# Attention then gMLP on one core: the first batch's attention in two halves of the queries, with gMLP of its first 384 tokens dealt into the second half

## The chip, the cores and the metric

The kernel runs on one core of a Trainium2 chip. The metric is the device time of one execution in microseconds (us). A profiled execution has a span, which was shorter than its time (224.21 and 221.9 us in the profile of the kernel before). TensorE is called PE, VectorE DVE, ScalarE ACT, GpSimd POOL, SyncE SP; PEld is the weight load of PE, and "SPq" is the queue into which SyncE puts transfers.

## The reference

Four batches, eight heads, 768 tokens, head size 64. Block-sparse attention (32-token blocks, a mask over 24 x 24 blocks), then a gMLP with spatial gating on its output.

```python
scores = q @ k.T / sqrt(D)                       # per batch and head, 768 x 768
attn   = softmax(where(mask, scores, -1e9)) @ v  # mask by blocks of 32
x      = attn as (batch, 768, 8 * 64)
h      = relu(x @ w_in)                          # 512 -> 1024
u, v   = h[..., :512], h[..., 512:]
v_n    = (v - mean(v)) / sqrt(var(v) + 1e-6)     # over 512
v_s    = einsum('ts,bsd->btd', w_spatial, v_n) + b_spatial
out    = (u * v_s) @ w_out                       # 512 -> 512
```

The spatial product takes all 768 tokens of a batch, so it must wait for the whole in-projection; the in-projection itself goes by 128 tokens.

## The kernel before

Everything is in bfloat16 on PE. The mask is part of the score product: rows 64 to 87 of a transposed key or query ("mask rows") hold a block indicator and the mask's row, so that 88 rows are contracted in place of 64. The scores come out transposed (keys on partitions), so the exponential feeds the value product directly. One pass of the main loop is a *slot*: two score matmuls, one exponential of 128x768, six value matmuls for a slot seven passes older. A head takes six slots, a pair of heads twelve, a batch 48.

```python
def qk_exp(j, ci):                                # head j, key chunk ci
    ps = psum.tile([128, 1024], FP32, tag="sc", bufs=2)
    for hf in range(2):                           # both halves of the queries
        nc.tensor.matmul(out=ps[:, hf * 512:hf * 512 + HALF],
                         lhsT=kt[j % 4][:, ci * 128:(ci + 1) * 128],
                         rhs=qt[j % 4][:, hf * HALF:(hf + 1) * HALF], ...)
    nc.scalar.activation(out=a_ref[j][:, ci, :]..., in_=ps..., func=AF.Exp, scale=0.125)

for p in range(NP + 1):                           # 16 pairs of heads
    for s in range(12):
        qk_exp(j, ci)
        ...                                       # transposes of pair p + 1
        if p == 0 and s == 0:
            cast_v(0); prepare(1); load(2); load_weights(2)
        if s == 7 and p + 2 < NP:
            if p + 3 < NP:
                load(p + 3)                       # three transfers of 0.39 MB
            ...
            prepare(p + 2)                        # POOL casts keys, queries, values to bf16
        if s == 10 and NG + 1 < p + 2 < NP:
            tr_dma(p + 2, "k"); tr_dma(p + 2, "q")  # transposes by DMA, same SPq
        ...                                       # from p = 5 on DVE copies the halves of pair p + 1, s = 5 and 9
        while moe_q and budget >= 0.5:            # gMLP matmuls of the batch before
            moe_q.popleft()(); budget -= 1
        if g >= LAG: av(...)
        if s == 8 and p >= NG:
            xtr(p - 1)
            if p % NG == 0:
                moe_q.extend(moe_units(p // NG - 1))   # 108 matmuls of 128x512
```

The mask rows of heads 1 to 3 are copied by DVE, and later heads reuse the same four tiles, mask rows included. All loads but the first two (the keys of heads 0 and 1, which ACT issues), all DMA transposes (keys, attention output, spatial weights, gates) and all stores are put into the one SP queue in program order.

The softmax here doesn't subtract the row's maximum and nothing guards it: scores larger than these inputs give would overflow.

## Time and profile before

| | before |
|---|---|
| time, median of 4 runs (lowest to highest) | 223.41 us (223.16 to 223.70) |
| span of the profiled execution | 221.9 us |
| mean granted clock of PE | 0.996 to 1.0 |

Two lines of the page of the kernel before that the prediction doesn't show. Each digit is a fortieth of the span (5.5 us): busy tenths of PE, then the granted clock of PE in tenths (9 is 90% or more).

```profile
PE   7999999999999999999999999999999999999993
...
PEclk9999999999999999999999999999999999999999
```

After the first slice PE is busy for nine tenths or more of every slice but the last, and the trace's clock record stays at 1.0 from 6.3 to 221.3 us. The second view is the table by stretches of the same trace, for the start; the columns are: stretch and its length, busy us and number of instructions of PE, PEld, DVE, ACT and POOL, granted clock, DMA share, GB/s.

```profile
9.00:10.50 1.50, 1.08 (x8) 0.63 (x7) 0.38 (x2) 1.50 (x3) 1.01 (x2) 1.00 0.15 49
10.50:12.00 1.50, 1.50 (x19) 1.04 (x17) 0.55 (x1) 1.33 (x3) 1.36 (x2) 1.00 0.00 0
```

From 9 to 12 us the DMA engines do next to nothing (shares 0.15 and 0.00). The old start could wait with its next loads: pair 2 was not needed before slot 24.

### The profile page before, as it was taken

What the parts mean: (1) busy time and instruction counts of PE and PEld (TensorE: products, weight loads), DVE (VectorE), ACT (ScalarE), POOL (GpSimd) and SP (SyncE); (2) the same over time, 40 slices, a digit from 0 to 9 for tenths busy, and PEclk for the clock granted to TensorE, in tenths of its full rate; (3) what the DMA queues carried; (4) which work ended last, traced back from release to release, by engine and by line L of the source; (5) the groups of instructions that cost most, each with busy time, mean ns of one, the idle gap of its engine ahead of it and who ended that gap; (6) DMA issues with size and microseconds to landing.
All of it is one profiled execution on the core that took longest, in us unless ns stands there. A gap on an engine that the chain in (4) does not pass through costs nothing.

```text
span 221.9 us, 5325 instructions
## 1 busy us (share of the span) xinstructions
PE 214.8 (97%) x2154; PEld 130.2 (59%) x2154; DVE 127.8 (58%) x282; ACT 177.1 (80%) x246; POOL 64.0 (29%) x88
## 2 busy tenths in 40 slices
PE   7999999999999999999999999999999999999993
PEld 3567777775656565665656555566656655544541
DVE  5566454557868545268867544559675433666531
ACT  5699999998899888888899878888989884265351
POOL 5436760439905701210606102110501000022000
PEclk9999999999999999999999999999999999999999
DMA  6679989996799886999774378998141124710015
GB/s 197 229 250 370 393 300 327 366 149 73 204 279 180 252 120 171 212 294 285 239 154 168 68 114 243 188 300 234 24 85 35 34 41 89 257 48 0 0 60 225
DMA packets 56092, 40.25 MB, mean 181 GB/s; under 512 B 39300, under 2 KB 51588, under 8 KB 56068
## 3 DMA queue, kind: packets, MB, share of 16 engines
q1 hardware_dynamic: 55780, 39.53, 67.7%
q10 hardware_dynamic: 288, 0.39, 0.6%
q8 instruction: 16, 0.26, 0.5%
q14 instruction: 8, 0.07, 0.1%
HBM read 24.38 MB, written 6.29 MB: 138 GB/s over the span
## 4 chain that ended last, share of the span: by engine, by line
PE 81%; ACT 14%; DVE 2%; issue 1%; POOLq 0%; POOL 0%
PE ps_moe L386 31%; PE ps L290 23%; ACT a_all L294 13%; PE ps_av L306 13%; PE ps_t L386 6%; PE ps_sc L386 3%; PE wps L180 2%; PE ps L228 1%; PE ps_x L330 1%; PE ps_g L434 1%; POOLq L567 0%; DVE gn L441 0%; DVE stats L399 0%; PE ps_tr L239 0%; ACT vsb L394 0%
## 5 line engine op out<-in xcount | busy, mean ns | idle before, releaser
L294 ACT ACTIVATE a_all<-ps 128x768 bf16<-128x768 f32 x192 | 149.5, 814 | 19.3 <-PE ps L290 10.7
L290 PE MATMUL ps<-qt,kt 88*128 88x384 bf16 x384 | 93.6, 325 | 1.8 <-ACT a_all L294 0.6
L306 PEld LDWEIGHTS <-a_all 128*128 128x128 bf16 x1152 | 60.4, 97 | 37.0 <-issue 0.4
L306 PE MATMUL ps_av<-vv,a_all 128*128 128x65 bf16 x1152 | 67.9, 194 | 0.0
L386 PE MATMUL ps_moe<-w_in_t,xt 128*128 128x512 bf16 x144 | 42.1, 378 | 0.0
L386 PE MATMUL ps_moe<-vn,w_spt 128*128 128x512 bf16 x108 | 31.8, 378 | 0.0
L290 PEld LDWEIGHTS <-kt 88*128 88x128 bf16 x384 | 28.2, 98 | 4.7 <-issue 1.9
L386 PEld LDWEIGHTS <-xt 128*128 128x128 bf16 x192 | 18.6, 97 | 16.1 <-issue 0.3
L112 POOL CAST vv<-st_v 128x768 bf16<-128x768 f32 x16 | 13.2, 828 | 47.3 <-PE ps_av L306 42.5
L441 DVE SCALAR_TENSOR_TENSOR gn<-ps_moe,b_col,un 128x512 bf16<-128x512 f32 x18 | 13.5, 748 | 18.6 <-PE ps_moe L386 18.5
L403 POOL TENSOR_SCALAR std<-mv 128x3 f32<-128x3 f32 x8 | 2.2, 277 | 72.2 <-DVE mv L400 59.5
L386 PE MATMUL ps_moe<-w_out_t,gt 128*128 128x512 bf16 x72 | 20.6, 378 | 0.1
L386 PEld LDWEIGHTS <-w_spt 128*128 128x128 bf16 x144 | 13.7, 97 | 11.4 <-issue 0.9
L399 DVE BATCH_NORM_STATS2 stats<-vsb 128x6 f32<-128x512 bf16 x24 | 16.7, 694 | 3.3 <-ACT vsb L394 2.7
L320 DVE TENSOR_TENSOR xn<-ps_av,rc 128x384 bf16<-128x384 f32 x32 | 17.8, 557 | 1.1
L396 DVE TENSOR_SCALAR vsb<-ps_moe 128x512 bf16<-128x512 f32 x18 | 12.4, 689 | 10.3 <-PE ps_moe L386 10.3
L109 POOL CAST nat_k<-st_k 128x768 bf16<-128x768 f32 x15 | 12.4, 825 | 17.4 <-DMA st_k<-in_k_dram 9.4
L319 DVE RECIPROCAL rc<-ps_av 128x6 f32<-128x6 f32 x32 | 6.0, 188 | 15.9 <-PE ps_av L306 15.8
L386 PEld LDWEIGHTS <-gt 128*128 128x128 bf16 x96 | 8.8, 97 | 6.9
L109 POOL CAST nat_q<-st_q 128x768 bf16<-128x768 f32 x15 | 12.5, 833 | 0.0
L409 DVE TENSOR_SCALAR vn<-vsb,mv,rstd 128x512 bf16<-128x512 bf16 x24 | 10.3, 447 | 2.6 <-POOL rstd L405 2.5
L279 DVE COPY kt<-tt_k 64x768 bf16<-64x768 bf16 x20 | 8.5, 425 | 4.2 <-DMA tt_k<-nat_k 4.1
(80 smaller groups left out, 172.7 us busy)
## 6 DMA issues: line engine op xcount, KB each, us to landing
st_v<-in_v_dram SPq DMA_DIRECT2D x16, 384.0 KB, 5.7
out_dram<-osb SPq DMA_DIRECT2D x24, 256.0 KB, 2.5
st_q<-in_q_dram SPq DMA_DIRECT2D x15, 384.0 KB, 3.8
st_k<-in_k_dram SPq DMA_DIRECT2D x15, 384.0 KB, 4.8
wst<-in_moe_w_spatial_dram SPq DMA_DIRECT2D x3, 768.0 KB, 8.5
wst<-in_moe_w_in_dram SPq DMA_DIRECT2D x4, 512.0 KB, 8.9
wst<-in_moe_w_out_dram SPq DMA_DIRECT2D x2, 512.0 KB, 7.2
st_k<-in_k_dram ACTq DMA_DIRECT2D x2, 192.0 KB, 3.0
```

Of the source, the lines that this page charges most:

```text
L109: eng.tensor_copy(out=dst, in_=src)
L112: nc.gpsimd.tensor_copy(out=vv[p % 3][:, :, :, 0:D], in_=st.pop(("v", p)).rearrange("p h (c d) -> p h c d", d=D))
L279: nc.vector.tensor_copy(out=(qt if nm == "q" else kt)[(2 * p + h) % 4][0:D, :], in_=src[h * D:(h + 1) * D, :])
L290: nc.tensor.matmul(out=ps[:, hf * 512:hf * 512 + HALF], lhsT=kt[j % 4][:, ci * 128:(ci + 1) * 128], rhs=qt[j % 4][:, hf * HALF:(hf + 1) * ...
L294: nc.scalar.activation(out=a_ref[j][:, ci, :].rearrange("p (b c) -> p b c", b=2), in_=ps.rearrange("p (b c) -> p b c", b=2)[:, :, 0:HALF], ...
L306: nc.tensor.matmul(out=av_ref[j][:, qc, :], lhsT=a_ref[j][:, ci, qc * 128:(qc + 1) * 128], rhs=vv[p % 3][:, h, ci, :], start=(ci == 0), st ...
L320: nc.vector.tensor_tensor(out=xn_ref[p][:, :, h, :], in0=ps[:, :, 0:D], in1=rc.to_broadcast([128, NCH, D]), op=ALU.mult)
L386: nc.tensor.matmul(out=box[0], lhsT=lhs, rhs=rhs, start=(i == 0), stop=(i == n - 1))
L396: nc.vector.tensor_scalar(out=vsb[:, tcc, :], in0=ps, scalar1=0.0, scalar2=None, op0=ALU.max)
L399: nc.vector.bn_stats(out=stats, in_=vsb[:, tcc, :])
L409: nc.vector.tensor_scalar(out=vn[:, tcc, :], in0=vsb[:, tcc, :], scalar1=mv[:, tcc, 0:1], scalar2=rstd[:, tcc:tcc + 1], op0=ALU.subtract, ...
L441: nc.vector.scalar_tensor_tensor(out=gn[:, tcc, :], in0=ps, scalar=b_col[:, tcc:tcc + 1], in1=un[:, tcc, :], op0=ALU.add, op1=ALU.mult)
```

## The change

The intent: the first batch is bound by ACT, and PE has gaps in it. If the eight heads are run for the first 384 queries, then for the second 384, three token chunks of the attention output are ready after 24 slots. Sixteen matmuls of the in-projection can then fill gaps of PE in the first batch, and so leave the stage that PE bounds.

```diff
+    def qk_exp_half(g):                           # 3 slots a head, 24 slots a half
+        gh, i = divmod(g, NCH // 2)
+        grp, j = divmod(gh, H)
+        ...
+        for u in range(2):
+            ci = 2 * i + u                        # two key chunks, one half of the queries
+            nc.tensor.matmul(out=ps[:, u * 512:u * 512 + HALF],
+                             lhsT=kt[j][:, ci * 128:(ci + 1) * 128],
+                             rhs=qt[j][:, grp * HALF:(grp + 1) * HALF], ...)
     ...
-    qt = [const.tile([KR, S], BF16, name=f"qt{s}") for s in range(4)]
+    qt_all = const.tile([KR, H, S], BF16)         # all eight heads of a batch are kept
+    qt = [qt_all[:, h] for h in range(H)]         # (keys and values likewise)
     ...
-        gt = work.tile([128, NCH, NDH, 128], BF16, tag="gt", bufs=2)
+        gt = work.tile([128, NCH, NDH, 128], BF16, tag="gt", bufs=1)
     ...
+        order = ("v0 v1 u0 v2 u1 u2 v3 v4 u3 v5 u4 u5" if b == 0 else
+                 "v0 v1 v2 v3 v4 v5 u0 u1 u2 u3 u4 u5" if last else
+                 "v0 v1 u0 v2 u1 v3 u2 v4 u3 v5 u4 u5")    # before: v0 v1 v2 u0 v3 u1 ...
     ...
+    for t in (kt_all, qt_all):                    # mask rows of heads 2 to 7, SBUF to SBUF
+        nc.sync.dma_start(out=t[D:KR, 2:H, :],
+                          in_=t[D:KR, 0:1, :].to_broadcast([NB, H - 2, S]))
+    load(2, "kq")
+    load_weights(1)
+    load(2, "v")
+    load(3, "kq")
+    load_weights(1)
+    load(3, "v")
     ...                                           # the first batch has a loop of its own:
+    for g in range(N0):                           # 48 slots
+        qk_exp_half(g)
+        for p, nm, third in tr_slots.get(g, ()):  # transposes of pairs 1 to 4
+            tr_pair(p, nm, third)
+        ...
+        if g == 30:
+            moe_q.extend(moe_units(0))
+        if g in (31, 32, 33, 34, 42, 43, 45, 46):
+            moe_q.popleft()()
+            moe_q.popleft()()
+        first_batch_rest(g)                       # value matmuls, 4 slots behind
```

## The prediction

> **What bounds the kernel now.** I speak of slots: one slot is one pass of the main loop, with two score matmuls (keys by queries), one exponential over 128x768, and six value matmuls for an older slot. Each batch has 48 slots, 192 in all; the gMLP of a batch is 108 matmuls of 128x512, dealt one to three at a time into the slots of the next batch.
>
> I read the page first: its busy shares and its 40 slices.
>
> ```profile
> PE 214.8 (97%) x2154; PEld 130.2 (59%) x2154; DVE 127.8 (58%) x282; ACT 177.1 (80%) x246; POOL 64.0 (29%) x88
> ...
> ACT  5699999998899888888899878888989884265351
> ```
>
> On average TensorE (PE) looks like the bound, but a mean mixes stages. ACT is at nine tenths in slices 3 to 9, so I asked for the busy time of each engine in two stretches, the first batch and the one after it.
>
> ```profile
> core 0: us, PE busy (x) PEld busy (x) DVE busy (x) ACT busy (x) POOL busy (x), PEclk, DMA share, GB/s
> 18.00:48.00 30.00, 29.41 (x408) 22.27 (x406) 15.25 (x32) 29.77 (x42) 13.70 (x16) 1.00 1.01 328
> 51.00:75.00 24.00, 24.00 (x247) 14.39 (x246) 18.46 (x40) 21.49 (x31) 15.82 (x15) 1.00 0.98 197
> ```
>
> In the first, ACT has no room; PE's 29.41 is modelled ends, not work. The chain that ended last says which engine times each stage (start, duration, what):
>
> ```profile
> 30.77 4.21 ACT a_all L294 x6
> 35.02 4.21 ACT a_all L294 x6
> ...
> 50.92 0.33 PE ps L290 x2
> 51.25 0.65 PE ps_moe L386 x3
> 51.90 0.19 PE ps_av L306 x6
> 52.09 0.33 PE ps L290 x2
> 52.42 0.43 PE ps_moe L386 x2
> 52.85 0.19 PE ps_av L306 x6
> ```
>
> Up to about 50 us the exponentials follow each other every 4.21/6 = 0.70 us, whereas PE needs 0.33 + 0.19 = 0.52 us a slot, and 0.11 more where two transposes lie in it. From 50 us on PE is the chain without a gap: score pair 0.33, value group 0.19, gMLP matmul 0.215 each (0.65/3). So the kernel is **ACT-bound for 57 slots, PE-bound after that**, to the end. A gMLP matmul moved from the second stage into an empty place of the first saves 0.215 us.
>
> How empty is the first stage? These are three successive slots of its timeline:
>
> ```profile
> 47.51 0.49 PE L290 MATMUL ps<-qt,kt 88*128 88x384 bf16 x2
> 47.83 0.36 PE L306 MATMUL ps_av<-vv,a_all 128*128 128x65 bf16 x6
> 48.21 0.49 PE L290 MATMUL ps<-qt,kt 88*128 88x384 bf16 x2
> ```
>
> A score pair is complete 0.49 after its start, an exponential alone takes 0.81, and there are two score buffers. So scores of slot n may start when exponential n-2 ends: 0.49 + 0.81 + some 0.05 of signalling = 1.35, against two periods of 0.705 = 1.41. PE can therefore run late by only some 0.06 us before ACT waits.
>
> [...]
>
> **The change part by part.**
>
> The first batch's 48 exponentials stay 48 of 128x768, but two key chunks by 384 queries in place of one by 768. So all heads' first halves are ready after 24 slots, and 16 gMLP matmuls (value columns of three token chunks, gate columns of one) can lie in slots 31 to 34, 42, 43, 45, 46.
>
> (a) Those 16 leave the PE-bound stage: 16 x 0.2155 = 3.45 us saved. In the first stage such a slot takes 0.33 + 0.19 + 0.43 = 0.95 on PE, 0.246 over the exponential's 0.706. Eight times 0.246 = 1.97, less 0.06 of room in each of three runs, is 1.8 us paid. Net gain **1.65**. It is nothing else than eight idle gaps of 0.185 filled.
>
> (b) The rest is dealt from slot 54 on, where before it began in slot 57. Before, the scores of slots 54 and 57 started at 47.51 and 49.80, with the six transposes of the fourth pair (0.33) between. PE's own work there is 3 x 0.52 = 1.56, and the transposes now lie in ACT-bound slots. Gain 2.29 - 1.56 = **0.7**. A 0.25 us gap of ACT at 43.6, for a probability buffer, should go too, as value matmuls now follow at 4 slots in place of 7: **0.2**.
>
> (c) Start: a head now takes three slots, so pairs 1 to 3 must be loaded, cast and transposed by slot 18. Slots 0 to 3 carry 12 to 14 small transposes and fillers more than an exponential covers; working them through, each loses 0.15 to 0.3, and exponential 6 starts at some 13.2, as before. Before, slot 12 lost a further 0.45 to a query copy. Gain **0.2**. The loads: 2.36 MB of the first two pairs, 0.44 of mask rows copied in SBUF, then keys and queries of pair 2, one weight piece, values 2, keys and queries of pair 3: 5.3 MB. At 328 to 374 GB/s from 2.2 us on that lands between 16.4 and 18.4, and the cast (0.83) follows; slot 13 comes at 18.2. Loss **0.3** as a mean of none and 0.6.
>
> (d) The instruction order shows a new wait. The second-half in-projection of slot 42 takes the PSUM buffer that the transposed queries of the next pair have just filled in slot 41; two copies of 0.56 must empty it. The copies end 0.44 + 0.2 + 1.12 = 1.76 after that slot's start; PE would be there after 1.13. So 0.6 to 0.7 is lost, and in slot 54 again 0.75, by the same order. Loss **1.4**.
>
> (e) One relu (0.48 behind an exponential, half covered) joins ACT in its own stage, and slots 8, 10, 14, 16 and 41 hold 0.03 to 0.1 too much transposing: loss **0.4**.
>
> (f) The remaining 92 matmuls over 51 slots make 0.52 + 1.8 x 0.2155 = 0.91 us a slot, where before it was 1.0. ACT needs 0.706 plus a relu of 0.48 every 2.2 slots in the in-projection, 0.92. The two are level there, and with two buffers that costs a little: loss **0.3**.
>
> (g) The last gMLP does all value columns first. Before, PE waited there 0.20 us for the normalised values; gain **0.2**. Eight more normalisations on DVE (8 x 0.3) and the single gate-transpose buffer are off the path: DVE was 51% busy from 18 to 48 us.
>
> Sum: 1.65 + 0.7 + 0.2 + 0.2 + 0.2 = 2.95 gained; 0.3 + 1.4 + 0.4 + 0.3 = 2.4 lost. Net 0.55. The slot list looks tuned by hand, so I trust the losses a little less than the gains and choose 1.5: **222.0 us**.
>
> **The rivals.** *The saving comes whole.* If PE had more room in the first stage than 0.06 us of lateness allows, the move would give up to 3.45 + 0.9, and the time would be near 219. For it: PE's 0.52 against 0.70. Against it: each burst holds four or two slots in a row, and only two score buffers exist.
>
> *A copy takes the place of the wait.* If the copies behind the query transposes queue up behind others on DVE, each costs over 1 us, and the gain is gone: 223.5 or more. For it: the order in (d). Against it: DVE is idle half the time.
>
> *The loads become the bound.* All four pairs must be there by 18 us. A late pair stalls PE and ACT together; 2 us late makes 224 to 225. For it: the DMA share is near 1 from 8 us on. Against it: the first 10 us carry the same bytes, sorted better (keys before values), and the weights come after.
>
> **Range and chances.** Of the gains, (a) and (b) are near certain; (c) to (f) each may be off by 0.5 to 1. Together some 1.6 us either way: 219.8 to 224.3. Over 2% faster needs 4.5 us, more than (a) and (b) can give without losses: 0.04. Over 2% slower needs a load over 4 us late: 0.02. Within 2%: 0.94.
>
> **What would show it.** In the changed kernel's chain, ACT should carry the slots up to 30; PE and ACT should mix in 31 to 46. The scores of slot 54 should start between 48.5 and 50 us (47.51 before). The waits list should show PE or its weight loads waiting for a query copy, about 0.6 us, twice. The row of exponentials should keep its 192 and 814 ns. From slot 54 to the end PE should be without gaps beyond 0.5 us in sum. I am wrong if PE waits for loads before 20 us for over 1 us, if exponentials stay 0.70 apart through slots 31 to 46 (then the saving is whole), or if the PE-bound stage shows gaps for weights or transposed gates.

## The result, and the profile after

| | before | after |
|---|---|---|
| time, median of 4 runs | 223.41 us (223.16 to 223.70) | 231.26 us (229.47 to 232.37) |
| ratio of the fast runs | | 1.034 [1.027, 1.042] |
| mean granted clock | 0.996 to 1.0 | 0.984 to 0.993 |

A ratio is the mean time of one kernel's fast runs over that of the other's fast runs of the same rounds, so it is not quite the ratio of the medians quoted; a 95% interval stands in brackets. The change made the kernel **slower by 3.4%**, outside the range of the prediction.

The page of the changed kernel:

```profile
PE 215.5 (95%) x2154; PEld 129.7 (57%) x2154; DVE 136.5 (60%) x297; ACT 178.1 (78%) x247; POOL 64.5 (28%) x89
...
PE   7979999998999999979999799999999999999992
...
ACT  5677999898999889886989678888999885266351
PEclk9997999999999999999999999999999999999999
```

The work is the same (215.5 us busy against 214.8), but PE has weak slices where it had none: slices 3, 10, 18 and 23; and in slice 4 the granted clock falls to seven tenths on average. ACT is less full in slices 3 and 4. The two stretches that the prediction read, of the changed kernel:

```profile
18.00:48.00 30.00, 28.96 (x360) 20.25 (x359) 17.38 (x49) 27.74 (x39) 12.04 (x14) 0.96 0.82 297
51.00:75.00 24.00, 23.26 (x248) 14.26 (x245) 20.72 (x35) 22.40 (x33) 19.36 (x17) 1.00 0.83 168
```

ACT has lost 2.0 us of the first (27.74 against 29.77) and PE, which had no gap in the second, 0.74. Where is it lost? I cut the execution at the starts of exponentials number 31 and 54. These starts are read from the trace; the forecast by stage is the prediction's own sum, divided among the stages by me ((c) and half of (e) to the first; the payment in (a), the first wait of (d), the other half of (e) and the ACT gap of (b) to the second; the rest to the third).

| | start to slot 31 | slots 31 to 54 | slot 54 to the end | span |
|---|---|---|---|---|
| before | 31.5 | 16.6 | 173.8 | 221.9 |
| forecast | 31.8 | 19.05 | 170.5 | 221.35 |
| after | 34.8 | 19.0 | 173.9 | 227.7 |

The middle is as forecast to within 0.1 us. In part that is luck: going by the middle stages of e9_late (18.3) and e14_nodeal (16.3) below, the gMLP slots cost 2.0 us where 1.8 was forecast and the wait 0.7 where 0.65 was, and the stage without either is 0.3 us shorter than before, where no difference was forecast. The profiled execution lost 3.0 us more than forecast in the start and 3.4 us in the long stage, where the saving should have come in. (The other three runs took 1.1 to 2.9 us longer than the profiled one; more on the clock below.)

**The start.** The same table by stretches as for before:

```profile
9.00:10.50 1.50, 1.50 (x16) 1.01 (x15) 1.47 (x3) 1.20 (x2) 0.83 (x1) 1.00 1.04 201
10.50:12.00 1.50, 1.47 (x20) 1.07 (x18) 1.35 (x4) 1.13 (x2) 0.83 (x1) 1.00 0.99 152
12.00:13.50 1.50, 1.35 (x22) 0.96 (x19) 1.44 (x3) 1.50 (x3) 0.46 (x1) 1.00 1.07 214
13.50:15.00 1.50, 0.81 (x10) 0.52 (x10) 0.12 (x2) 0.76 (x2) 0.37 (x1) 1.00 1.07 362
15.00:18.00 3.00, 2.28 (x27) 1.62 (x26) 1.38 (x4) 2.03 (x3) 1.65 (x2) 0.79 1.04 384
18.00:21.00 3.00, 3.00 (x35) 2.29 (x34) 2.00 (x6) 2.16 (x3) 2.21 (x3) 0.64 1.05 387
```

From 9 to 13.5 us the DMA engines are full (share 0.99 to 1.07), yet move only 152 to 214 GB/s; afterwards they move 362 to 387 at the same share. In the slow stretch the mask rows are being copied from SBUF to SBUF (the two transfers are put into the queue at 6.55 and 7.62 us, and PE's wait for them ends at 14.19). Then the clock: 0.79 and 0.64 on average, and the trace's clock record has 0.5 from 16.73 to 20.14 us. What PE waited for, from its timeline (start, duration, what, idle time before and what ended it):

```profile
14.19 0.48 PE L319 MATMUL ps<-qt_all,kt_all 88*128 88x384 bf16 x2 [0.83 <-DMA qt_all<-qt_all]
...
15.91 0.28 PE L242 MATMUL ps_tr<-ident,nat_k 128*128 128x128 bf16 x2 [0.72 <-POOL nat_k L110]
...
44.10 0.60 PE L432 MATMUL ps_moe<-w_in_t,xt 128*128 128x512 bf16 x2 [0.53 <-DVE qt_all L247]
...
54.33 0.60 PE L432 MATMUL ps_moe<-w_in_t,xt 128*128 128x512 bf16 x2 [0.63 <-DVE qt_all L247]
...
91.44 0.59 PE L432 MATMUL ps_moe<-w_out_t,gt 128*128 128x512 bf16 x2 [0.78 <-DVE gn L490]
...
102.63 0.51 PE L376 MATMUL ps_x<-ident,xn 128*128 128x128 bf16 x6 [1.33 <-DVE xn L366]
...
127.52 0.38 PE L432 MATMUL ps_moe<-vn,w_spt 128*128 128x512 bf16 x1 [0.86 <-DVE vn L455]
128.35 0.38 PE L432 MATMUL ps_moe<-vn,w_spt 128*128 128x512 bf16 x1 [0.45 <-DVE vn L455]
```

The first wait is for the mask rows of slot 6, the second for the cast keys of pair 2. The two at 44 and 54 us are the waits for query copies that the prediction foresaw. The last four, 3.42 us in sum, are those that the long stage lacks.

**The long stage.** The waits at 91 and 103 us name DVE. So I looked at what DVE did just before the second of them:

```profile
101.16 0.72 DVE L273 COPY kt_all<-tt_k 64x768 bf16<-64x768 bf16 x2 [3.12 <-DMA tt_k<-nat_k]
...
102.02 0.56 DVE L366 TENSOR_TENSOR xn<-ps_av,rc 128x384 bf16<-128x384 f32 x1
```

DVE had been standing for 3.12 us in front of a copy of transposed keys (tt_k) that had not landed; the normalisation that PE needed came after it in program order. The chain that ended last shows what held the keys:

```profile
84.60 4.68 DMA tt_k<-nat_k
...
91.83 4.16 DMA st_k<-in_k_dram
...
96.27 4.87 DMA tt_k<-nat_k
```

A load (put into the queue at 91.83), its cast, then the transpose of the keys: transfers are on the path, in a stage in which PE alone was expected there. The load came late because it stood in the SP queue behind transposes of gates, keys and queries (issued from 83.2 to 91.2 us), which themselves waited for DVE and POOL: from 74 to 92 us the queue had waits of 2.1 and 1.7 us for DVE's key and query copies and of 1.9 us for a cast of POOL. In the waits list POOL's wait for keys grew from 9.4 us (6 times, longest 4.6) before to this:

```profile
POOL nat_k L110 <- DMA st_k<-in_k_dram: 39.6, 6, 15.6
...
DVE kt_all L273 <- DMA tt_k<-nat_k: 8.0, 3, 3.1
```

The wait at 127 us is of another kind. The in-projection's new order puts the value columns of the last chunks later, so they are normalised later. DVE then does one normalisation (0.90 us from 123.95), two copies of keys (1.87 from 124.76) and two more normalisations (1.65 from 126.65), and PE, which goes straight on to the spatial product, waits for these.

### The profile page after: what moved, and what is told of

Same layout as the page of the kernel before. It is cut to its first block, busy times and chain, and to the rows that moved or that the text cites.

```text
span 227.7 us, 5347 instructions
## 1 busy us (share of the span) xinstructions
PE 215.5 (95%) x2154; PEld 129.7 (57%) x2154; DVE 136.5 (60%) x297; ACT 178.1 (78%) x247; POOL 64.5 (28%) x89
## 4 chain that ended last, share of the span: by engine, by line
PE 66%; DMA 11%; DVE 6%; issue 6%; ACT 4%; POOL 4%; SPq 1%; POOLq 0%; ACTq 0%
PE ps_moe L432 23%; PE ps L284 14%; PE ps_av L300 8%; DMA st_k<-in_k_dram 7%; PE ps_t L432 7%; PE ps L319 6%; DMA tt_k<-nat_k 4%; PE ps_sc L432 3%; PE ps_av L335 3%; ACT a_all L323 3%; DVE kt_all L273 1%; ACT a_all L288 1%; POOL nat_k L110 1%; PE ps_tr L242 1%; DVE vn L455 1%
## 5 line engine op out<-in xcount | busy, mean ns | idle before, releaser
L284 PE MATMUL ps<-qt_all,kt_all 88*128 88x384 bf16 x288 | 70.3, 325 | 0.1
L300 PEld LDWEIGHTS <-a_all 128*128 128x128 bf16 x864 | 46.1, 97 | 34.9 <-issue 1.1
L432 PE MATMUL ps_moe<-w_in_t,xt 128*128 128x512 bf16 x144 | 42.7, 378 | 1.2 <-DVE qt_all L247 1.2
L432 PE MATMUL ps_moe<-vn,w_spt 128*128 128x512 bf16 x108 | 32.5, 378 | 1.3 <-DVE vn L455 1.3
L432 PEld LDWEIGHTS <-xt 128*128 128x128 bf16 x192 | 18.4, 97 | 17.4 <-DVE qt_all L247 1.9
L319 PE MATMUL ps<-qt_all,kt_all 88*128 88x384 bf16 x96 | 24.3, 335 | 1.4 <-DMA qt_all<-qt_all 0.8
L490 DVE SCALAR_TENSOR_TENSOR gn<-ps_moe,b_col,un 128x512 bf16<-128x512 f32 x18 | 13.5, 748 | 17.1 <-PE ps_moe L432 17.1
L455 DVE TENSOR_SCALAR vn<-vsb,mv,rstd 128x512 bf16<-128x512 bf16 x24 | 17.7, 768 | 4.9 <-POOL rstd L451 4.9
L284 PEld LDWEIGHTS <-kt_all 88*128 88x128 bf16 x288 | 19.3, 98 | 0.6 <-issue 0.2
L113 POOL CAST vv<-st_v 128x768 bf16<-128x768 f32 x16 | 13.5, 842 | 16.7 <-PE ps_av L335 9.9
L335 PEld LDWEIGHTS <-a_all 128*128 128x128 bf16 x288 | 15.2, 100 | 4.7 <-issue 0.2
L366 DVE TENSOR_TENSOR xn<-ps_av,rc 128x384 bf16<-128x384 f32 x24 | 13.4, 558 | 0.8
(91 smaller groups left out, 221.3 us busy)
```

The source lines that it names most:

```text
L113: nc.gpsimd.tensor_copy(out=vv[p % NG][:, :, :, 0:D], in_=st.pop(("v", p)).rearrange("p h (c d) -> p h c d", d=D))
L284: nc.tensor.matmul(out=ps[:, hf * 512:hf * 512 + HALF], lhsT=kt[j % H][:, ci * 128:(ci + 1) * 128], rhs=qt[j % H][:, hf * HALF:(hf + 1) * ...
L300: nc.tensor.matmul(out=av_ref[j][:, qc, :], lhsT=a_ref[j][:, ci, qc * 128:(qc + 1) * 128], rhs=vv[p % NG][:, h, ci, :], start=(ci == 0), s ...
L319: nc.tensor.matmul(out=ps[:, u * 512:u * 512 + HALF], lhsT=kt[j][:, ci * 128:(ci + 1) * 128], rhs=qt[j][:, grp * HALF:(grp + 1) * HALF], s ...
L335: nc.tensor.matmul(out=av_ref["half", gh][:, qc, :], lhsT=a_ref["half", gh][:, ci, qc * 128:(qc + 1) * 128], rhs=vv[p][:, h, ci, :], start ...
L432: nc.tensor.matmul(out=box[0], lhsT=lhs, rhs=rhs, start=(i == 0), stop=(i == n - 1))
```

## The experiments

Eighteen kernels ran, in five lots, each lot on one chip together with runs of the kernel before. Ratios are to the kernel before in the same lot. Four repairs come up several times; I name them here:

- *loads*: from pair 9 on the loads are put into the queue five slots earlier.
- *order*: the in-projection order of before (v0 v1 v2 u0 v3 ...) for the second and third gMLP.
- *transposes*: those of pairs 4 and 5 are dealt one slot earlier at their end, so that their copies are over before the gMLP wants the PSUM buffer.
- *mixed start*: mask rows of heads 2 and 3 by four DVE copies, those of heads 4 and 5 by transfers behind the keys of pair 2, those of 6 and 7 behind the keys of pair 3, and the first weight piece after that.

### First lot: where the losses are

**a_again**: the changed kernel once more.

> The changed kernel itself, on the chip of the three experiments beside it. Theory: 6 to 9 us slower than before; a low-clock stretch of about 3.4 us (one or two of them) at half the clock before 25 us, and TensorE gaps of 0.8, 1.3 and 1.3 us near 91, 103 and 128 us. If the low clock were an accident of the first chip, this run would lack it and be only some 4 us slower than before.

It took 231.13 us, 1.034 [1.030, 1.039], with the wait for mask rows now 2.29 us and the late waits within 0.3 us of those above. The result stands; the size of the wait at the start varies from run to run.

**e1_mask**: mask rows of heads 2 to 7 by twelve DVE copies in place of the two transfers.

```diff
-    for t in (kt_all, qt_all):
-        nc.sync.dma_start(out=t[D:KR, 2:H, :], in_=t[D:KR, 0:1, :].to_broadcast(...))
+        if g in (3, 5, 8, 11, 14, 17):
+            j = (3, 5, 8, 11, 14, 17).index(g) + 2
+            for t in (kt, qt):
+                nc.vector.tensor_copy(out=t[j][D:KR, :], in_=t[0][D:KR, :])
```

> Mask rows of heads 2 to 7 by twelve small vector copies in place of the two SBUF-to-SBUF transfers. Theory (the two transfers hold the queue from 9.5 to 13 us at half its rate, so mask rows and the keys of pair 2 come late, TensorE idles, and its clock is halved): the 0.8 and 0.7 us waits go, keys of pair 2 land near 12.5 instead of 15 us, no half-clock stretch, the scores of slot 12 start near 18 instead of 20.6 us, and the time falls by 3 to 5 us. Rival (the loads themselves are too many for the first 18 us, the transfers matter little): under 1 us.

It took 230.65 us, 1.029 [1.023, 1.035]. Its profiled run fell in the slow state, so of it I use only what was waited for and when keys were cast, not the length:

```profile
15.43 0.50 PE L319 MATMUL ps<-qt_all,kt_all 88*128 88x384 bf16 x2 [0.98 <-DVE qt_all L568]
...
26.32 0.34 PE L356 MATMUL ps_x<-ident,xn 128*128 128x128 bf16 x3 [1.65 <-DVE xn L347]
```

The keys of pair 2 were now cast at 11.92, 3.1 us earlier, but the copies made DVE the one that PE waits for. A miss in its effect (0.5 us off a_again's median, where 3 to 5 were expected), yet it shows that the transfers held the keys of pair 2. The keys of pair 3 came no earlier: cast at 20.25, against 19.47 in the changed kernel.

**e2_fill**: four matmuls of 512 columns on zeros before each of the two early waits, so that PE is not idle there.

> The transfers stay; four filler matmuls of 512 columns stand before each of the two early waits, so TensorE is busy while it waits. If the halved clock comes of the idle stretch at 13 to 16 us: full clock throughout, the waits themselves remain, and the time falls by 1.3 to 3 us. If the clock is lowered by something else (the rise of all engines' load, or chance): the half-clock stretch stays and the time rises by 0 to 1 us.

It took 229.53 us, 1.029 [1.024, 1.033]. The clock was 0.996 to 1.0 in all four runs, against 0.981 to 0.993. The stretch that had 0.79 (the next, with 0.64 before, has 1.00 too):

```profile
15.00:18.00 3.00, 2.53 (x26) 1.44 (x25) 0.54 (x2) 1.51 (x2) 1.28 (x2) 1.00 1.04 386
```

So **the halved clock follows from PE's idle time at the start** (1.55 us of the 3.4 us ahead of it in the changed kernel), and is worth about 0.5% (1.034 to 1.029, 1.2 us; the intervals overlap). It is a consequence, not the first cause.

**e3_loads**: the *loads* repair alone.

```diff
-                if p + 3 < NP:
+                if p + 3 < NP and p < 6:
                     load(p + 3)
+            if s == 2 and p >= 6 and p + 3 < NP:
+                load(p + 3)
```

> From the seventh pair on, the loads of a pair are issued five slots earlier, ahead of the transposed stores of gated rows in the same queue. Theory (loads stand behind those in the queue, the transposed keys come late, VectorE waits for them in order, and TensorE for VectorE): the TensorE gaps near 91 and 103 us (0.8 and 1.3) go, the start stays as it is, and the time falls by 2 us. Rival (the transfers of this stretch are simply too many, the order is no matter): the gaps move elsewhere, the time stays within 0.5 us.

It took 229.72 us, 1.026 [1.021, 1.032]. The waits at 91 and 103 us are gone, and DVE's wait for transposed keys fell from 8.0 to 1.5 us, as the theory says. The waits at 127 and 128 us are still 0.86 and 0.45. The time fell by 1.4 us from a_again, where 2 was expected.

### Second lot: the other late waits, and the dealing itself

**e4_order**: the *order* repair alone.

> The in-projection order of the second and third gMLP as in the kernel before (three value chunks ahead of the first gate chunk, and three gate chunks after the last value chunk, in place of two and two). Theory: the TensorE gap near 128 us (0.86 + 0.45, normalised values not there) goes, as 4 more matmuls stand between the last value chunk and the spatial product; the time falls by 1.3 us. Rival (the values are late because of the key copies on VectorE and the casts on GpSimd, not the order): the gap stays or moves, under 0.4 us.

It took 229.87 us, 1.024 [1.017, 1.031]. No PE wait is left at 127 us; those at 91 and 102 us stay. That settles this pair of waits.

**e5_tr**: the *transposes* repair alone.

```diff
-                     (3, (13, 14, 14, 15, 16, 16)), (4, (36, 37, 38, 39, 40, 41))):
+                     (3, (13, 14, 14, 15, 16, 16)), (4, (36, 37, 37, 38, 39, 40))):
```

(and in the same way for pair 5)

> The transposes of the fifth and sixth pair end one slot earlier, so that their copies out of PSUM are over when the in-projection wants the buffer. Theory: the waits of 0.53 and 0.63 us near 44 and 54 us go and the time falls by 1.0 to 1.4 us. Rival (ACT is the bound there and takes the gap anyway): under 0.4 us.

It took 231.03 us, 1.031 [1.026, 1.036]. The waits of 0.53 and 0.63 us at 44 and 54 us are gone, but its profile has a longer wait at the start than any other:

```profile
17.13 0.80 PE L319 MATMUL ps<-qt_all,kt_all 88*128 88x384 bf16 x2 [3.66 <-DMA qt_all<-qt_all]
```

So the time of this run says little about the repair; the waits do.

**e6_nodeal**: no gMLP in the first batch; all 108 matmuls from slot 54 on.

```diff
-        if g in (31, 32, 33, 34, 42, 43, 45, 46):
-            moe_q.popleft()()
-            moe_q.popleft()()
```

> No gMLP in the first batch: all 108 matmuls of the first gMLP are dealt from slot 54 on; the halves stay. By the prediction's own sum the 16 moved matmuls are worth 3.45 - 1.8 - 0.7 - 0.25 = 0.7 us, so the scores of slot 54 start 2.7 us earlier and the time rises by 0.7. If the moving is also what causes the late transposed keys at 91 and 103 us (everything of the first gMLP stands earlier in the transfer queue), those 2 us come back and the time falls by 1 to 1.5 us. If the moved matmuls lay in idle time for nothing, the time rises by 3 us.

It took 231.21 us, 1.033 [1.025, 1.041]: no different from the changed kernel. The waits at 91 and 103 us are gone here too (the gMLP is not ahead, so the keys are in time), those at 128 us are not. That the dealing was worth nothing here does not yet say what it is worth when nothing stands in its way (e14).

**e8_split**: the mask rows of heads 2 and 3 first, those of heads 4 to 7 behind the keys of pair 2.

> The mask rows of heads 2 and 3 alone go ahead of the loads of pair 2, those of heads 4 to 7 behind its keys and queries. No work is added to VectorE. Theory (the two transfers run at half rate and hold up the first rows and the keys behind them): the wait before slot 6 falls from 0.8 to 2.3 us to under 0.5, the keys of pair 2 land 1.5 to 2 us earlier, the scores of slot 12 start 1.5 to 2.5 us earlier, one or both half-clock stretches go, and the time falls by 2 to 4 us. Rival (the bytes have to come through before slot 12 anyway): the wait moves to slots 7 to 13, under 1 us.

It took 230.91 us, 1.032 [1.025, 1.038]. The wait before slot 6 is gone, but the one for cast keys has moved on to pair 3 and is longer:

```profile
22.55 0.29 PE L242 MATMUL ps_tr<-ident,nat_k 128*128 128x128 bf16 x2 [2.81 <-POOL nat_k L110]
```

Splitting the transfers moves the loss and does not take it away, as long as four heads' mask rows and a weight piece stand ahead of the keys of pair 3.

### Third lot: repairs together

**e9_late**: *loads*, *order* and *transposes*; the start as changed.

> The three repairs behind slot 36 together (loads earlier, old in-projection order, transposes a slot earlier); the start as changed. If the losses add, ratio 1.034 - 0.008 (loads) - 0.008 (order) - 0.003 (transposes) = 1.015, or 227 us, and no TensorE gap over 0.3 us after 40 us. What is then left over the kernel before, some 3.5 us, is the start alone, and the scores of slot 54 start 3 to 5 us later than before's 47.5. If the repairs overlap (the same time, counted twice), ratio over 1.02.

It took 227.7 us, 1.014 [1.006, 1.023]. After 40 us PE has no wait over 0.42 us. At the start it waits 2.71 us for mask rows and 0.86 for cast keys. So the late repairs give about 3.4 us (231.1 to 227.7, over two lots).

**e10_latemask** and **e11_latemask_all** (results wrong): scores of heads 2 to 7 with 64 rows, that is without mask rows in the first pass, and the two transfers not issued until slot 34; in the second with the three late repairs.

> Wrong results on purpose: in the first batch heads 2 to 7 are taken without the mask rows (64 rows in place of 88), and the two transfers that make them run at slot 34, for the later batches. This takes the transfers out of the start without giving VectorE anything. Theory (the transfers are what delays the start): no wait before slot 6, keys of pair 2 cast near 12.5 us, full clock, scores of slot 12 near 18 us, time down by 3 to 4 us. Rival (the loads of pairs 2 and 3 are too many for the time whatever the mask rows do; in e1_mask the keys of pair 3 landed at 20.2 us without the transfers): a wait for the keys of pair 3 at slot 13 of 1 to 2 us, time down by 1 to 2 us only.

> Wrong results on purpose, as e10_latemask, with the three repairs of e9_late. What the change would be worth if the mask rows cost nothing. By the prediction's sum with (d), the late loads and the in-projection order taken out: 223.4 - 2.9 + 0.7 = 221 us, if the start is no slower than before. If the start still loses 2 us to the loads: 223.

They took 230.88 us, 1.030 [1.019, 1.041], and 227.17 us, 1.012 [1.002, 1.021]. The granted clock was 1.0 in their profiles, but PE took longer for a slot with score matmuls of 64 rows: in e10_latemask, at 12.3 us, a score pair and a value group take 0.41 and 0.30 us from start to start, in place of the 0.33 and 0.19 of 88 rows (slots 0.84 to 0.95 apart from 13 to 18 us). So the gain of the start was lost in another way, and for the time these two are inconclusive. The rival's sign did come in e10_latemask: without any mask rows in the start PE still waited 1.01 us for the cast keys of pair 3, cast at 18.79. For the cause they are useful all the same. The trace records each packet of a transfer; loads and mask rows go in packets of 1536 bytes. Their median duration:

| stretch | before | after | e2_fill | e10_latemask | mixed start (e12) |
|---|---|---|---|---|---|
| 8 to 10 us | 65 ns | 65 | 65 | 65 | 65 |
| 10 to 12 us | none | 155 | 160 | 65 | 65 |
| 12 to 14 us | 65 | 98 | 141 | 65 | 65 |
| 14 to 16 us | 65 | 68 | 75 | 65 | 65 |
| 30 to 32 us | 66 | 65 | 66 | 193 | 68 |

The long packets go where the six-head transfers go: at 10 to 14 us in the changed kernel, at 30 to 32 us where they are issued at slot 34. **While the mask rows are copied, the median packet takes 1.5 to 3 times as long.** In the changed kernel 421 of the 661 packets of this size from 9 to 14 us took over 100 ns (before: 10 of 385). The mask rows are only 288 packets (2 transfers of 216 KB), so at least 133 of the long ones belong to loads. Summed over the packets between 6 and 26 us that took over 100 ns, the excess over 65 ns is 2.3 us of all 16 engines in the changed kernel (2.9 in its second profile) and 0.6 us before. The sum alone does not decide the start: it is 1.6 in e12_mix and 2.4 in e13_xfer below, whose starts are repaired.

**e12_mix**: *mixed start* with the three late repairs.

```diff
+    def mask_dma(h0):
+        for t in (kt_all, qt_all):
+            nc.sync.dma_start(out=t[D:KR, h0:h0 + 2, :],
+                              in_=t[D:KR, 0:1, :].to_broadcast([NB, 2, S]))
     load(2, "kq")
-    load_weights(1)
+    mask_dma(4)
     load(2, "v")
     load(3, "kq")
+    mask_dma(6)
+    load_weights(1)
     ...
+        if g in (1, 5):
+            j = 2 if g == 1 else 3
+            for t in (kt, qt):
+                nc.vector.tensor_copy(out=t[j][D:KR, :], in_=t[0][D:KR, :])
```

> Right results. Mask rows of heads 2 and 3 by four vector copies, those of 4, 5 and 6, 7 by transfers of two heads each, behind the keys of pair 2 and of pair 3; a weight piece moves behind the keys of pair 3; the three repairs of e9_late. If the start can be repaired by order: 1.5 to 2.5 us better than e9_late, near 224.5 us. If bytes and not order are the limit of the start: within 0.7 us of e9_late.

It took 223.89 us, 1.000 [0.991, 1.009], with a right result: 1.5% less than e9_late of the same lot, from the start alone. Keys of pair 2 were cast at 11.58 (after: 15.03), those of pair 3 at 17.75 (after: 19.47). PE was left with these waits over 0.3 us:

```profile
97.27 0.51 PE L376 MATMUL ps_x<-ident,xn 128*128 128x128 bf16 x6 [0.71 <-DVE xn L366]
```

and 0.76 us at 13.44 for a query copy, and 0.63 at 109.11 for a relu of DVE.

### Fourth lot: what of the start, and what the dealing is worth

**e13_xfer**: as e12_mix, but the mask rows of heads 2 and 3 by two-head transfers ahead of the keys of pair 2, not by DVE.

> As the mixed version (1.000 of before), but the mask rows of heads 2 and 3 come by two two-head transfers ahead of the keys of pair 2, not by four VectorE copies. If what matters is how many bytes stand ahead of the keys (0.15 MB here, 0.44 MB in the changed kernel), it stays within 0.3% of the mixed version, near 224. Rival, the start is repaired by taking the transfers of mask rows away from in front of the keys altogether: 225.5 or more, with a wait for cast keys of over 1 us before slot 6 or 12.

It took 224.84 us, 1.002 [0.996, 1.007]. That is within the noise of e12_mix; the longest wait for cast keys is 0.60 us, so the rival with over 1 us falls. It does not take DVE: two heads' mask rows may stand ahead of the keys. What this does not separate is the weight piece (0.52 MB, more than the mask rows' 0.44), which the *mixed start* also moves behind the keys of pair 3; no run moves it alone.

**e14_nodeal**: as e12_mix, without gMLP matmuls in the first batch.

> The mixed version without gMLP matmuls in the first batch: all 108 from slot 54 on. By part (a) of the prediction the dealing is worth 1.65 us net once nothing else is in the way, so this should be 1.65 us slower than the mixed version of the same sort, near 225.5 (1.007 of before). Rival, the dealing is worth nothing (the slots of the first batch with gMLP pay for it all): equal, 223.9. Second rival, the saving is whole: 227.3.

It took 224.46 us, 0.999 [0.994, 1.005]. My expectation of 1.65 us against the mixed version was missed: there is no difference. The stages, below, tell why.

**e15_best**: as e12_mix, with the early loads four slots earlier still for all later pairs, and the copies of the transposed keys at s = 7 in place of 5.

> The mixed version with the loads of the pairs from 9 on issued at the end of the slot groups before (four slots earlier than at slot 2), and the copies of the transposed keys two slots later. If the gaps at 97 and 109 us (0.71 and 0.63) are VectorE held by a late transposed key, they go and it takes 222.5 to 223 (0.995 of before). If they come from VectorE's own load, they stay or move, and it takes 223.9 as before.

It took 226.04 us, 1.007 [1.002, 1.013]. The waits at 97 and 109 us are gone, as expected if late keys held DVE. But the time, expected at 222.5 to 223, was missed, as a new wait took their place:

```profile
146.41 0.61 PE L432 MATMUL ps_moe<-w_out_t,gt 128*128 128x512 bf16 x2 [2.02 <-DMA gt<-gn]
```

**e16_start**: the changed kernel with the *mixed start* alone.

> The changed kernel with the start alone repaired as in the mixed version (mask rows of heads 2 and 3 by copies, the others behind the keys of pairs 2 and 3), and none of the three later repairs. If start and later gaps are independent: 231.2 - 3.8 = 227.4 to 228 (1.019). If the later gaps follow from the late start: 224 to 225, and the gaps at 91 and 103 us shrink.

It took 227.87 us, 1.017 [1.012, 1.021], as the first theory had it (227.4 to 228). **Start and late losses add up**: three of the late waits are the old ones (1.33, 0.86, 0.45 us), though everything began earlier; that at 91 us shrank to 0.24.

### Fifth lot: the wait in e15, and what remains

**e17_two**: as e15_best, with the still earlier loads for pairs 9 to 12 only.

```diff
             if s == 10 and p + 2 < NP:
                 tr_dma(p + 2, "k")
                 tr_dma(p + 2, "q")
+                if p in (5, 6, 7, 8):
+                    load(p + 4)
+            if s == 2 and p >= 10 and p + 3 < NP:
+                load(p + 3)
```

> The version with earlier loads and later key copies, but the early loads only for pairs 9 to 12; from pair 13 on they stay at slot 2. If the 2.02 us wait for a transposed gate at 146 us came of the loads standing ahead of that transfer in the one queue, it goes, and the time is 2 us less than with them: 224.0 against 226.0, 0.998 of before in its own job. If it came of the single gate buffer, the wait stays.

It took 223.10 us over 22 runs, 0.996 [0.993, 0.998]. The wait for the transposed gate is gone with the same single gate buffer, so that wait came of the loads ahead of the transfer in the one queue. After 26 us PE has no wait over 0.2 us.

**e18_kqfirst**: the same, with keys and queries of pair 3 ahead of the values of pair 2, in the queue and in POOL's casts.

> The same, and keys and queries of pair 3 ahead of the values of pair 2, in the queue and in the casts. If bytes ahead of the keys are what the first 20 us lack, the wait for cast keys of pair 3 (1.27 us at 19.6 in the run before) goes: 1 us less than its twin, 223.0, and 0.994 of before. Rival, the values of pair 2 are now late and the wait moves to slot 16: equal to its twin.

It took 222.66 us, 0.994 [0.992, 0.996]: the **fastest of all, 0.6% less than the kernel before**, and 0.1% less than its twin, which the intervals don't separate. (The interval leaves out 1.) The start has no wait over 0.3 us any more. The wait of 1.27 us on which the expectation rested was in e15_best's profile; that of the twin has only one of 0.51 us, for a query copy, so this pair doesn't test the order of pair 3's keys. One new wait has come, 1.11 us at 76.32 for a transposed piece of the spatial weights, once more a transfer from the same queue.

### The stages of the repaired kernels

Starts of exponentials from each profile, cut as above, in us:

| | start to slot 31 | slots 31 to 54 | slot 54 to the end | span |
|---|---|---|---|---|
| before | 31.5 | 16.6 | 173.8 | 221.9 |
| after | 34.8 | 19.0 | 173.9 | 227.7 |
| e16_start | 33.4 | 19.0 | 173.2 | 225.6 |
| e12_mix | 32.3 | 18.2 | 170.8 | 221.3 |
| e14_nodeal | 34.8 | 16.3 | 172.9 | 224.0 |
| e17_two | 33.5 | 18.3 | 169.5 | 221.3 |
| e18_kqfirst | 32.1 | 18.3 | 170.5 | 220.9 |

Against e14_nodeal, e17_two pays 18.3 - 16.3 = **2.0 us** in slots 31 to 54 and gains 172.9 - 169.5 = **3.4 us** after: 1.4 us net from the dealing, in stages where neither has a wait over 0.2 us for data. (They are of two lots and differ in the loads too, so this is a reading of stages, not a pair made for it.) e12_mix gains only 2.1 of it, since its two waits of 0.71 and 0.63 us are not in e14_nodeal, and 2.1 - 1.9 is nothing that the times could show. The first stage is not that steady: e14_nodeal, with the same start as e12_mix, had in its profile a wait of 1.59 us for the keys of pair 3 and a halved clock.

Part of the first column is not the kernels' own, either. The clock record of a profile begins some way into the span (at 6.26 us before, with 1.0), and the mean granted clock counts no loss ahead of it: in the profile of before it is 1.00 for 2 to 6 us, though six transposes of one shape took 0.85 us at 4.69 and 0.52 at 6.75. In six profiles (e1_mask, e2_fill, e8_split, e9_late, e16_start, e17_two) it begins at 10.2 to 10.5 us, in the others at 3.9 to 6.5. In e17_two, one of the six, a score pair took 0.85 us at 8.69, and 0.50 at 10.36; in e18_kqfirst, one of the others, 0.50 at 7.89. In the six the first exponential starts at 9.57 or 9.58 us, in the others between 7.45 and 8.58. So 1.1 of the 1.4 us between the starts of e17_two and e18_kqfirst were there before the first slot. Before and after (8.46 and 8.58) are not touched by it.

## Why the prediction was wrong

It said 222.0 us, in 219.8 to 224.3; it was 231.3. By its own steps:

- **(a) held, as far as stages show it.** Four of the gMLP slots start 0.95 us apart, as computed:

```profile
34.24 0.48 PE L319 MATMUL ps<-qt_all,kt_all 88*128 88x384 bf16 x2
34.56 0.60 PE L432 MATMUL ps_moe<-w_in_t,xt 128*128 128x512 bf16 x2
34.99 0.35 PE L335 MATMUL ps_av<-vv,a_all 128*128 128x65 bf16 x6
35.19 0.49 PE L319 MATMUL ps<-qt_all,kt_all 88*128 88x384 bf16 x2
```

  It put 1.8 us as paid and 3.45 as saved; the repaired kernels show 2.0 and 3.4. In the changed kernel itself the saving was eaten, and no pair of times shows it (e12_mix against e14_nodeal: no difference).
- **(d) held**: two waits for query copies, 0.53 and 0.63 us (0.65 and 0.75 predicted). Together with (a), (b) and (e) the middle stage came to 19.0 us, forecast 19.05.
- **(c) is the step that failed first.** It took 0.44 MB of mask rows as bytes like any others, at 328 to 374 GB/s (in the trace before, the rates from 18 to 48 and from 26 to 30 us), and had all keys land by 18.4 us for a loss of 0.3. Its sign for this was a wait of over 1 us for loads before 20 us; the waits were 0.83 and 0.72, 1.55 us together. The runs show 152 to 214 GB/s for 4.5 us, packets of 112 to 171 ns (medians of the stretches from 9 to 13.5 us) in place of 65, the keys of pair 3 cast only from 19.5 us on, and a start 3.0 us longer than forecast (3.9 in the second profile). The step priced a transfer of a new kind with the rate of another kind; no row of the kernel before showed a plain copy from SBUF to SBUF. How much of the loss is the mask rows' and how much that of the weight piece ahead of pair 3's keys, no run separates.
- **Its third rival, the loads as the bound, was right in kind** but given 224 to 225 us. The line that it read for that rival was false: the DMA share is not near 1 from 8 us on in the kernel before; it is 0.15 and 0.00 from 9 to 12 us. So "the same bytes, sorted better", which it held against the rival, missed the point: the old start had 3 us of empty queue where the new one has its worst congestion, and one weight piece does not come after. Idle PE then cost the clock on top (0.79 and 0.64 from 15 to 21 us; 1.00 with the fillers of e2_fill), a term that the sum doesn't have at all.
- **The sum had no term for the second loss**, 3.4 us of waits from 91 to 129 us. The prediction said that PE would have no gaps beyond 0.5 us there. It looked at the gMLP as 92 matmuls over 51 slots, and not at the transfers that the gMLP puts into the queue. Dealt earlier, they stand ahead of the loads, the keys are transposed late, and DVE, in program order, holds up the normalisation that PE needs. e3_loads takes away the waits at 91 and 103 us, e4_order those at 127. The line of the prediction that names what would make it wrong, "gaps for weights or transposed gates", was in the right place with the wrong tile.
- **(g)** called the single gate buffer off the path. e17_two shows that it is, with the transfers in a good order. Its 0.2 us for the last gMLP I did not measure apart; the wait of 0.20 us at 204 us before is gone after. A normalisation 192 wide took 0.357 us, where it counted 0.3, an estimate of its own (384 wide took 0.557 before).
- **(b) and (f)**: e17_two has 169.5 us after slot 54, 1.0 less than forecast; 0.75 of that is the second wait of (d), which its *transposes* repair takes away. So (f), 0.3 us for ACT level with PE, was not too small; I can't divide the rest.

Of the loss of 3.4%, the *mixed start* gives back 1.8% (1.034 to 1.017, over two lots), the three late repairs a further 1.7% (1.017 to 1.000), the better order of the loads 0.4 to 0.6%. With all of them the change is worth 1.3 us (223.96 against 222.66). That this is close to the 1.5 us (223.5 to 222.0) that the prediction chose is partly luck: with the waits of (d) repaired, its own sum would be 0.55 + 1.4 = 1.95. And the repairs of the loads were not tried on the kernel before, so not all of the 1.3 need be the change's. The prediction was right about the exchange between the two stages, and wrong to take it that the transfers would keep up.

The range has a slip of its own: 222.0 with "1.6 us either way" is 220.4 to 223.6, not 219.8 to 224.3. And over 2% slower, which came true, had a chance of 0.02, tied to a load over 4 us late; no such load was needed.

What stays open: why the packets lengthen while rows are copied within SBUF. In these copies one source row is read six times, and all of it comes from and goes to 24 partitions; whether either has to do with it, no run tells. With two-head transfers the median stays at 65 ns up to 18 us in e12_mix, but reaches 89 to 93 ns in e13_xfer (10 to 12, 14 to 16 and 18 to 20 us) and 166 with four heads in e8_split (14 to 16 us).

Open too: how much idle time of PE brings the halved clock. Ten of the twenty profiles show one before the kernel's last microseconds. In the 3.4 us just ahead of the first halving PE was idle for 1.55 us (after), 1.59 (e14_nodeal), 1.77 (e1_mask) and 2.02 to 2.66 us (the other seven). But stretches of the same length with up to 1.95 us of it passed without one in e2_fill, and one with 1.69 in e15_best, in its wait of 2.02 us. Ends of matmuls are modelled; what decides between 1.55 and 1.95 us, no run here shows.

## What to carry to other kernels

Before you pull work forward, list what it brings into a shared queue, and look what stands behind it there (a load four or five slots later or earlier made waits of 0.7 to 2.0 us on PE come and go in e3_loads, e15_best and e17_two): the engine that a wait names may itself be standing in program order behind a late transfer, as DVE was here for 3.12 us. Price a transfer of a new kind only by one that a trace shows; what must land first goes into the queue first (keys of pair 2 were cast at 11.58 us in e12_mix, at 15.03 in the changed kernel). If a change of sound mechanism loses, cut both executions at the same slots and look for the stage that is off, then repair it there: here 3.4% slower became 0.6% faster.
